# RetNet retention and an ELU feed-forward block: a new order for the first 35 microseconds of work

## The chip, the cores and the metric

The kernel runs on one core of one Trainium2 chip. The metric is the device time of one execution in microseconds, taken over several runs, with the median as its summary. The trace is of one profiled execution. The engines appear in it as PE (TensorE, matrix products; PEld is its weight load), DVE (VectorE), ACT (ScalarE), POOL (GpSimd) and SP (the sync queue, which issues all the transfers here).

## What is computed

A recurrent retention over 4 batches, 8 heads, 768 positions and head size 64 is followed by a feed-forward block with an ELU on 3072 tokens (model width 512, hidden width 2048). All data are float32, and the two weight matrices come in as float64.

```python
for t in range(S):
    state = gamma * state + k[:, :, t] (outer) v[:, :, t]
    y[:, :, t] = scale * q[:, :, t] @ state
x = y.transpose(0, 2, 1, 3).reshape(B * S, H * D)
h = x @ w_in
g = np.where(h > 0.0, h, np.exp(np.minimum(h, 0.0)) - 1.0)
return g @ w_out
```

## The kernel before

The tokens go in six blocks of 512. A block has four chunks of 128 positions. For two chunks at a time (a pair `pp`), retention runs in four steps: `scores` makes k-q products (L265) and DVE masks them in place (L270); `states` makes k-v products (L287) and sums them into running states, the first by an ACT copy (L296), the others by DVE additions (L298); `outputs` multiplies masked scores with v (L311), then states with q (L335, in two halves between which DVE reads one column of each bank into a tile `seen`, L323), and DVE multiplies the result with a decay table `etab` into `xb` (L342). `scale_v` multiplies v by decay factors: chunks 1 and 3 in eight small ACT instructions (L236), chunks 0 and 2 in one DVE instruction (L239), later ones on GpSimd.

The feed-forward weights come as 16 pieces of 1 MB in float64 bits. `load_piece` (L118) brings a piece into one of three staging buffers. `prepare` gives it to ACT (two instructions, L139 and L141, for each part), `decode` to DVE (four instructions for each part, L160 to L163), and the decode of a piece also issues the load of the piece three further on. `prepare(parts)` cuts a piece into that many parts by columns; `decode` is a generator that stops behind each part. Pieces 0 to 7 are the halves `w_a[n]`, `w_b[n]` of the first weight matrix for n = 0 to 3, pieces 8 to 15 belong to the second one.

Block 0 is computed with plain products, since the later blocks use a seven-product scheme that needs combined weights. `plain_first` makes 16 tiles of 128 hidden units by 512 tokens: for each n two tiles of `w_a[n]` and two of `w_b[n]`. Four of them are done in two halves of 256 tokens (L385), the first halves as soon as pair 0 has left `xb`, the second halves behind pair 1. They take four accumulation banks, a, a, b and d. The other twelve take all 512 tokens at once (L396). Each float32 product appears as two PE instructions. `elu` runs on ACT (L373, L374) and closes on DVE (L376). In the loop over these tiles a further piece is decoded behind every second one. `plain_second` then makes the output product for block 0 with one piece of the second matrix in each of eight rounds f (L410); DVE makes four sums of the piece in each round (L415), and the next decode follows. Within these rounds the retention of block 1 is placed too.

There is no scheduler: the order in which the code emits instructions is the order on each engine. The opening is written out by hand at L711 to L742. All loads stand in one queue on SP. It first issues piece 0, chunks 0 and 1, piece 1, chunks 2 and 3, and piece 2 (L173 to L179); `load` sends a chunk's transposed q and k (`qk`), then its plain k and v (`kvn`), 0.5 MB each. Before the tile loop starts, pieces 0, 1 and 2 have been decoded, in two, one and two parts.

Of the kernel before, what the change touches and what calls it, by code (L numbers as in the profile page):

```python
# [10 lines left out]
U32 = mybir.dt.uint32  # L11
# [5 lines left out]
def kernel(  # L17
# [30 lines left out]
    nc = tc.nc  # L48
    PSUM = bass.MemoryType.PSUM
    P = nc.NUM_PARTITIONS  # L50
# [8 lines left out]
    NCHUNK = NTOK // C  # L59
# [32 lines left out]
    chunks = [divmod(m, NCH) for m in range(NCHUNK)]  # L92
    raw = {}

    def load(m):

        if m >= NCHUNK:
            return
        qk = ldpool.tile([P, 2, HP, C], FP32, name="qk", tag="qk")
        nc.sync.dma_start(qk.rearrange("p a h c -> p (a h c)"), qkv[m, :, 0:1024])  # L100
        kv = ldpool.tile([C, 2, H, D], FP32, name="kvn", tag="kvn")
        nc.sync.dma_start(kv.rearrange("p a h c -> p (a h c)"), qkv[m, :, 1024:2048])
        raw[m] = (qk, kv)

# [3 lines left out]
    NPIECE = 2 * NQ + NF  # L110
    staged, prepared, decoded = [], [], []

    def load_piece():
        n = len(staged)
        if n < NPIECE:

            t = stage.tile([P, 1024, 2], U32, name="wraw", tag="stage")
            nc.sync.dma_start(t.rearrange("p c w -> p (c w)"), w_bits[n].bitcast(U32))  # L118
            staged.append(t)


# [2 lines left out]
    def prepare(parts=1):  # L124

        n = len(prepared)
        if n >= NPIECE:
            return
        t = staged[n]
        if n < 2 * NQ:  # L130
            dst = (w_a, w_b)[n % 2][n // 2].rearrange("p a b c d -> p (a b c d)")
        else:

            dst = w_s[n % NQ].rearrange("p a b c d -> p (a b c d)")[:, 0:1024]
        todo = []
        for part in range(parts):
            c = slice(part * 1024 // parts, (part + 1) * 1024 // parts)
            lo, hi, flat = t[:, c, 0], t[:, c, 1], dst.bitcast(U32)[:, c]
            nc.scalar.activation(flat, lo, AF.Copy, scale=2.0**-29)  # L139

            nc.scalar.activation(lo.bitcast(FP32), hi.bitcast(FP32), AF.Abs)  # L141
            todo.append((lo, hi, flat))
        prepared.append((dst, todo))
# [5 lines left out]
    def decode():  # L149

        n = len(decoded)
        if n >= NPIECE:
            return
        dst, todo = prepared[n]
        decoded.append(dst.rearrange("p (a b) -> p a b", a=2))
        vec = nc.vector
        for c, hi, flat in todo:
            cf = c.bitcast(FP32)

            vec.tensor_scalar(cf, cf, 122879.9921875, 2.0**-15, ALU.min, ALU.max)  # L160
            vec.tensor_scalar(c, c, 3, 0x3FFFFFF8, ALU.logical_shift_left, ALU.bitwise_and)
            vec.scalar_tensor_tensor(c, hi, 0xC0000000, c, ALU.bitwise_and, ALU.bitwise_or)
            vec.tensor_tensor(out=flat, in0=c, in1=flat, op=ALU.add)  # L163
            yield
        load_piece()
        if n >= 2 * NQ:
            nc.sync.dma_start(quarters(n - 2 * NQ)[:, 0:8], dst.rearrange("p (s c) -> p s c", c=P))

    def decode_all():
        for _ in decode():  # L170
            pass

    load_piece()  # L173
    load(0)
    load(1)
    load_piece()
    load(2)
    load(3)
    load_piece()  # L179


# [13 lines left out]
    etab = const.tile([P, 2, 2, S], FP32, name="etab")  # L195
# [33 lines left out]
    def scale_v(m):  # L229
        if m >= NCHUNK:  # L230
            return
        i = chunks[m][1]
        qk, kv = raw[m]
        if m in (1, 3):
            for h in range(H):
                nc.scalar.activation(kv[:, 1, h, :], kv[:, 1, h, :], AF.Copy, scale=vf[:, i, h : h + 1])  # L236
            return
        eng = nc.vector if m < CPB else nc.gpsimd
        eng.tensor_tensor(  # L239
            out=kv[:, 1], in0=kv[:, 1], in1=vf[:, i].unsqueeze(2).to_broadcast([C, H, D]), op=ALU.mult  # L240
        )
# [11 lines left out]
    def fresh(tb, n):  # L253

        return (tb * 2 * CPB + n) % (S // D) == 0

    def scores(tb, pp):

        two = [raw[tb * CPB + 2 * pp + x][0] for x in range(2)]
        sc = [ps_r.tile([P, 2, HP, D], FP32, name="sc", tag="r") for _ in range(2)]  # L260
        for x, qk in enumerate(two):
            for p in range(HP):
                for sub in range(2):
                    for a in range(2):
                        nc.tensor.matmul(  # L265
                            sc[a][rows(sub), x, p, :], lhsT=qk[rows(a), 1, p, rows(sub)],
                            rhs=qk[rows(a), 0, p, rows(sub)], start=True, stop=True, skip_group_check=True,
                        )
        for a in range(2):
            nc.vector.tensor_tensor(  # L270
                out=two[a][:, 1].rearrange("p h c -> p (h c)").rearrange("p (n t) -> p n t", t=D),
                in0=sc[a].rearrange("p x h t -> p (x h) t"),
                in1=cmask.unsqueeze(1).to_broadcast([P, 2 * HP, D]), op=ALU.mult,
            )

    def states(tb, pp):

        kvs = [ps_r.tile([P, 2, HP, D], FP32, name="kv", tag="r") for _ in range(2)]
        order = [(x, sub) for x in range(2) for sub in range(2)]
        last = lambda x, sub: fresh(tb, 4 * pp + 2 * x + sub + 1)  # L280
        for x in range(2):
            kv = raw[tb * CPB + 2 * pp + x][1]
            for p in range(HP):
                for sub in range(2):
                    for a in range(2):
                        if not last(x, sub):
                            nc.tensor.matmul(  # L287
                                kvs[sub][rows(a), x, p, :], lhsT=kv[rows(sub), 0, 2 * p + a, :],
                                rhs=kv[rows(sub), 1, 2 * p + a, :], start=True, stop=True, skip_group_check=True,
                            )  # L290
        for x, sub in order:
            n = 4 * pp + 2 * x + sub
            if last(x, sub):
                continue
            if fresh(tb, n):
                nc.scalar.copy(state(tb, n + 1), kvs[sub][:, x])  # L296
            else:
                nc.vector.tensor_tensor(out=state(tb, n + 1), in0=kvs[sub][:, x], in1=state(tb, n), op=ALU.add)  # L298
# [67 lines left out]
    def flush():  # L366
        while later:
            later.pop(0)()
# [9 lines left out]
    def plain_first():  # L378

        tiles = [(n, w, row, fi) for n in range(NQ) for w, row in ((w_a, 0), (w_b, 1)) for fi in range(2)]  # L380
        banks = [bank(x) for x in "aabd"]
        for t in range(2):
            for (n, w, row, fi), hp in zip(tiles, banks):
                for j in range(4):
                    nc.tensor.matmul(  # L385
                        hp[:, t, :], lhsT=w[n][:, fi, j // 2, j % 2, :], rhs=xb[:, j, half[t]],
                        start=(j == 0), stop=(j == 3), skip_group_check=True,
                    )
                if t == 1:
                    elu(g_plain[row * NF + 2 * n + fi], hp.rearrange("p a b -> p (a b)"))  # L390
                if t == 1 or fi == 1:
                    yield
        for n, w, row, fi in tiles[4:]:
            hp = ps_r.tile([P, TB], FP32, name="hp", tag="r")
            for j in range(4):
                nc.tensor.matmul(  # L396
                    hp, lhsT=w[n][:, fi, j // 2, j % 2, :], rhs=xb[:, j, :], start=(j == 0), stop=(j == 3)
                )
            elu(g_plain[row * NF + 2 * n + fi], hp)
            yield  # L400
        flush()

    def plain_second():

# [37 lines left out]
    def bank(x):  # L442
        return ps_f.tile([P, 2, TH], FP32, name="p" + x, tag=x, bufs=2 if x == "a" else 1)
# [264 lines left out]
            pass  # L708


    prepare(2)  # L711
    piece = decode()
    next(piece)
    scale_v(0)
    scale_v(1)
    scores(0, 0)
    next(piece)
    next(piece, None)
    states(0, 0)
    prepare()  # L720
    y = outputs(0, 0)
    next(y)
    next(y)
    next(y, None)
    scale_v(2)
    decode_all()
    scale_v(3)
    prepare(2)
    inner = plain_first()
    next(inner)  # L730
    scores(0, 1)
    states(0, 1)
    piece = decode()
    next(piece)
    next(inner)
    y = outputs(0, 1)
    next(y)
    next(y)
    next(y, None)
    next(piece)  # L740
    next(piece, None)
    prepare()  # L742
    for n, _ in enumerate(inner):
        if n % 2 == 1 and n < 15:
# [139 lines left out]
```

## Time and profile before

| what | us |
|---|---|
| median of 8 runs | 667.08 |
| lowest and highest of them | 664.66, 668.96 |
| profiled execution, whole | 667.51 |
| profiled execution, span of the trace | 665.5 |
| PE, DVE, ACT busy in the span | 640.9, 435.2, 228.3 |

A busy PE isn't PE at its peak, since the ends of matmuls are modelled. The mean granted clock of PE was 0.994 of full speed. At the start of the span the transfers dominate: the first chunk's scores begin at 7.43 us, the first tile's products at 20.03 us, and the twelve tiles with 512 tokens at 43.09 us.

### The profile page before, as it was taken

Reading aid. Unit: us, or ns where it says so; the run is one execution under the profiler, and the core shown is the slowest. Engines: PE = TensorE matmul, PEld = TensorE weight load, DVE = VectorE, ACT = ScalarE, POOL = GpSimd, SP = SyncE. Lnnn points to the kernel's source line nnn. Section 1 sums busy time; section 2 is a strip of 40 time slices with the busy share of each in tenths; the row PEclk is TensorE's granted clock in tenths of the full one; section 3 lists DMA queues with packets and bytes.
Section 4 is the critical chain, followed back from the end, with each engine's and each line's share of the span. In section 5 each row is a group of like instructions: output and inputs, shape, how many; then the busy total and the mean of one; then the engine's idle time right before and its main releaser. Section 6 shows DMA issues by size and latency. Waiting matters only on the chain.

```text
span 665.5 us, 14662 instructions
## 1 busy us (share of the span) xinstructions
PE 640.9 (96%) x6144; PEld 539.8 (81%) x6144; DVE 435.2 (65%) x769; ACT 228.3 (34%) x432; POOL 25.1 (4%) x28
## 2 busy tenths in 40 slices
PE   4889999999999999999999999999999999999997
PEld 4664444548888888889989888999889989888996
DVE  5688768656767744548856447867447858355874
ACT  7467642105441002543112454112455111445211
POOL 1000100000200000200000300000200000000000
PEclk9799999999999999999999999999999999999999
DMA  9538978449214757605767703777801768301693
GB/s 344 227 127 303 320 223 261 129 134 367 100 50 155 261 218 254 252 1 168 217 202 254 255 1 94 224 230 249 299 0 50 230 197 272 95 1 30 203 307 126
DMA packets 63825, 123.64 MB, mean 186 GB/s; under 512 B 5136, under 2 KB 22544, under 8 KB 61712
## 3 DMA queue, kind: packets, MB, share of 16 engines
q1 hardware_dynamic: 63760, 122.70, 55.9%
q8 instruction: 49, 0.80, 0.5%
q14 instruction: 16, 0.13, 0.0%
HBM read 100.66 MB, written 22.02 MB: 184 GB/s over the span
## 4 chain that ended last, share of the span: by engine, by line
PE 87%; DVE 8%; issue 2%; DMA 1%; ACT 0%; SPq 0%; DVEq 0%
PE pa L497 20%; PE pa L618 12%; PE pd L497 9%; PE pd L618 7%; PE hp L396 6%; PE pb L497 5%; PE pa L410 4%; PE pa L555 4%; DVE ts L607 3%; PE pb L618 2%; PE pd L555 2%; PE pd L410 2%; PE pb L410 2%; PE y L335 2%; PE sc L265 2%
## 5 line engine op out<-in xcount | busy, mean ns | idle before, releaser
L452 DVE TENSOR_TENSOR h<-pd,m 128x512 f32<-128x512 f32 x42 | 29.1, 692 | 86.0 <-ACT m L447 68.5
L447 ACT COPY m<-pa 128x512 f32<-128x512 f32 x63 | 36.3, 577 | 109.7 <-PE pa L497 73.7
L626 ACT COPY ms<-pa 128x128 f32<-128x128 f32 x84 | 22.3, 266 | 129.1 <-PE pa L618 124.6
L618 PE MATMUL pd<-ts,wq 128*128 128x128 f32 x448 | 60.3, 278 | 2.9 <-DVE res L630 2.9
L374 ACT ACTIVATE r<-r 128x512 f32<-128x512 f32 x96 | 60.5, 630 | 3.0
L618 PE MATMUL pa<-ts,wq 128*128 128x128 f32 x448 | 59.2, 275 | 0.0
L618 PEld LDWEIGHTS pd<-ts,wq 128*128 128x128 f32 x448 | 54.4, 192 | 4.6 <-DVE res L630 4.3
L373 ACT ACTIVATE r<-h 128x512 f32<-128x512 f32 x60 | 37.9, 631 | 57.2 <-DVE h L452 57.2
L618 PEld LDWEIGHTS pa<-ts,wq 128*128 128x128 f32 x448 | 54.8, 192 | 0.2
L618 PE MATMUL pa<-gC,wq 128*128 128x128 f32 x384 | 52.0, 278 | 0.4 <-ACT ms L626 0.4
L376 DVE SCALAR_TENSOR_TENSOR gC<-r,h 128x512 f32<-128x512 f32 x60 | 42.1, 702 | 10.8 <-ACT r L374 10.8
L618 PEld LDWEIGHTS pa<-gC,wq 128*128 128x128 f32 x384 | 47.2, 192 | 1.7 <-ACT ms L626 0.5
L239 POOL TENSOR_TENSOR kvn<-kvn,vf 128x512 f32<-128x512 f32 x20 | 23.1, 1153 | 457.4 <-DMA kvn<-in_qkv_dram 397.6
L497 PE MATMUL pa<-xb,w_s 128*128 128x256 f32 x160 | 37.8, 379 | 0.0
L497 PE MATMUL pa<-xb,w_a 128*128 128x256 f32 x160 | 37.8, 379 | 0.0
L497 PE MATMUL pa<-xt,w_s 128*128 128x256 f32 x160 | 37.8, 379 | 0.0
L497 PE MATMUL pa<-xt,w_b 128*128 128x256 f32 x160 | 37.8, 379 | 0.0
L497 PE MATMUL pd<-xt,w_b 128*128 128x256 f32 x160 | 37.8, 379 | 0.0
L497 PE MATMUL pb<-xb,w_a 128*128 128x256 f32 x160 | 37.8, 379 | 0.0
L497 PE MATMUL pd<-xt,w_s 128*128 128x256 f32 x160 | 37.8, 379 | 0.0
L630 DVE TENSOR_TENSOR res<-pd,ms 128x128 f32<-128x128 f32 x56 | 16.1, 287 | 31.3 <-PE pd L618 29.5
L497 PEld LDWEIGHTS pa<-xt,w_b 128*128 128x128 f32 x160 | 30.4, 190 | 4.1
(121 smaller groups left out, 1098.0 us busy)
## 6 DMA issues: line engine op xcount, KB each, us to landing
wq<-scratch_dram SPq DMA_DIRECT2D x196, 256.0 KB, 4.0
wraw<-in_w_dram SPq DMA_DIRECT2D x16, 1024.0 KB, 5.8
qk<-in_qkv_dram SPq DMA_DIRECT2D x24, 512.0 KB, 8.8
kvn<-in_qkv_dram SPq DMA_DIRECT2D x24, 512.0 KB, 9.4
scratch_dram<-so SPq DMA_DIRECT2D x22, 512.0 KB, 3.3
ws<-scratch_dram SPq DMA_DIRECT2D x7, 1024.0 KB, 7.8
scratch_dram<-w_s SPq DMA_DIRECT2D x8, 512.0 KB, 7.4
out_dram<-res SPq DMA_DIRECT2D x12, 256.0 KB, 3.7
```

The lines of the kernel that those rows point to most:

```text
L239: eng.tensor_tensor(out=kv[:, 1], in0=kv[:, 1], in1=vf[:, i].unsqueeze(2).to_broadcast([C, H, D]), op=ALU.mult)
L373: nc.scalar.activation(r, h, AF.Relu, scale=-1.0)
L374: nc.scalar.activation(r, r, AF.Exp, scale=-1.0)
L376: later.append(lambda: nc.vector.scalar_tensor_tensor(g, r, -1.0, h, ALU.add, ALU.max))
L396: nc.tensor.matmul(hp, lhsT=w[n][:, fi, j // 2, j % 2, :], rhs=xb[:, j, :], start=(j == 0), stop=(j == 3))
L410: nc.tensor.matmul(ops[d], lhsT=wo[:, row, d * P : (d + 1) * P], rhs=g_plain[row * NF + f], start=(f == 0 and row == 0), stop=(f == NF - 1 ...
L447: nc.scalar.copy(m, ps)
L452: nc.vector.tensor_tensor(out=h, in0=ps, in1=m, op=ALU.add)
L497: nc.tensor.matmul(ps[:, fi, :], lhsT=w[:, fi, j2, :], rhs=x[:, j2, :], start=(begin and fi == 0 and j2 == 0), stop=(j2 == 1), skip_group_ ...
L555: nc.tensor.matmul(ps[:, d, :], lhsT=ws[:, 2 * d + f // 4, f % 4, :], rhs=gq[INPUT2[j]][:, f, :], start=(begin and f == 0 and d == 0), sto ...
L618: nc.tensor.matmul(ps, lhsT=w[:, f, :], rhs=ts[j][k][:, f, :], start=(begin and f == 0), stop=(f == 3), skip_group_check=True,)
L626: nc.scalar.copy(m, ps)
```

## The change

The load of a chunk is split into its two transfers, so that the queue can send qk of two chunks before kv of either. The first issues become: qk0, qk1, kv0, kv1, piece 0 as two halves, piece 1, qk2, qk3, kv2, kv3, piece 2. v of chunk 0 is scaled on ACT and that of chunks 1, 2 and 3 on DVE. Pieces 0 and 1 are prepared and decoded in four parts each, and these parts are placed between the steps of retention; piece 2 is prepared in one part and is decoded inside the tile loop. Two tiles instead of four are done in halves of 256 tokens, in the two a banks, with a stop behind each half tile, and fourteen are done whole. A new function `busy` multiplies two ranges of columns of `etab` into bank b; nothing reads the result. It is called four times in the first pair of chunks.

```diff
+    def load_qk(m):
+        qk = ldpool.tile([P, 2, HP, C], FP32, name="qk", tag="qk")
+        nc.sync.dma_start(qk.rearrange("p a h c -> p (a h c)"), qkv[m, :, 0:1024])
+        raw[m] = [qk, None]
+    def load_kv(m):
+        kv = ldpool.tile([C, 2, H, D], FP32, name="kvn", tag="kvn")
+        nc.sync.dma_start(kv.rearrange("p a h c -> p (a h c)"), qkv[m, :, 1024:2048])
+        raw[m][1] = kv
...
-    def load_piece():
+    def load_piece(parts=1):
...
-            nc.sync.dma_start(t.rearrange("p c w -> p (c w)"), w_bits[n].bitcast(U32))
+            for part in range(parts):
+                c = slice(part * 2048 // parts, (part + 1) * 2048 // parts)
+                nc.sync.dma_start(t.rearrange("p c w -> p (c w)")[:, c], w_bits[n].bitcast(U32)[:, c])
...
+    load_qk(0)
+    load_qk(1)
+    load_kv(0)
+    load_kv(1)
+    load_piece(2)
     load_piece()
-    load(0)
-    load(1)
-    load_piece()
-    load(2)
-    load(3)
+    load_qk(2)
+    load_qk(3)
+    load_kv(2)
+    load_kv(3)
     load_piece()
...
-        if m in (1, 3):
+        if m == 0:
...
-        banks = [bank(x) for x in "aabd"]
+        banks = [bank("a") for _ in range(2)]
...
-                if t == 1 or fi == 1:
-                    yield
-        for n, w, row, fi in tiles[4:]:
+                yield
+        for n, w, row, fi in tiles[2:]:
...
+    def busy(columns):
+        ps = bank("b").rearrange("p a b -> p (a b)")
+        nc.tensor.matmul(ps[:, 0:columns], lhsT=etab[:, 0, 0, 0:P], rhs=etab[:, 0, 1, 0:columns], start=True, stop=True)
...
-    prepare(2)
+    scale_v(0)
+    scores(0, 0)
+    scale_v(1)
+    prepare(4)
     piece = decode()
     next(piece)
-    scale_v(0)
-    scale_v(1)
-    scores(0, 0)
+    states(0, 0)
+    y = outputs(0, 0)
+    next(y)
+    busy(512)
+    busy(256)
+    next(y)
+    next(piece)
+    busy(256)
+    next(y, None)
+    busy(256)
+    next(piece)
     next(piece)
     next(piece, None)
-    states(0, 0)
-    prepare()
-    y = outputs(0, 0)
-    next(y)
-    next(y)
-    next(y, None)
-    scale_v(2)
-    decode_all()
-    scale_v(3)
-    prepare(2)
+    prepare(4)
+    piece = decode()
     inner = plain_first()
     next(inner)
+    scale_v(2)
     scores(0, 1)
+    scale_v(3)
+    next(inner)
+    next(piece)
     states(0, 1)
-    piece = decode()
-    next(piece)
-    next(inner)
     y = outputs(0, 1)
     next(y)
     next(y)
     next(y, None)
-    next(piece)
-    next(piece, None)
+    for _ in piece:
+        pass
     prepare()
```

## The prediction

> **What bounds the kernel now.** I read the chain of waits first, because it says which engine sets the end. TensorE holds 87% of it.
>
> ```profile
> PE 87%; DVE 8%; issue 2%; DMA 1%; ACT 0%; SPq 0%; DVEq 0%
> ```
>
> So only time in which TensorE is idle or slow can be won. The busy times by stage show where that is (columns: stretch, its length, then busy us and instructions of PE, PEld, DVE, ACT, POOL; granted clock, DMA share, GB/s).
>
> ```profile
> 0.00:18.50 18.50, 7.99 (x240) 7.47 (x240) 9.76 (x38) 11.97 (x21) 2.00 (x8) 1.00 0.91 352
> 18.50:25.60 7.10, 5.69 (x20) 4.48 (x14) 5.65 (x7) 4.78 (x13) 0.00 (x0) 0.52 0.73 278
> 25.60:43.30 17.70, 15.96 (x309) 13.72 (x308) 12.52 (x23) 6.64 (x9) 0.00 (x0) 1.00 0.33 118
> 43.30:84.40 41.10, 41.10 (x97) 18.15 (x96) 32.82 (x39) 28.79 (x39) 4.44 (x4) 1.00 0.84 287
> 84.40:148.50 64.10, 64.10 (x609) 31.77 (x608) 46.04 (x80) 14.25 (x15) 0.14 (x1) 1.00 0.61 182
> ```
>
> From 43.30 to 148.50 TensorE has no gap. All that the change can win lies ahead of 43.3, and nothing after it may be lost. The same chain in order of time (start, length, what) shows the opening's links:
>
> ```profile
> 2.11 7.86 DMA qk<-in_qkv_dram
> ...
> 16.75 1.36 issue
> ...
> 20.03 6.39 PE pa L385 x16
> ...
> 34.74 1.30 DVE xb L342 x2
> ...
> 36.08 3.72 PE pa L385 x16
> ```
>
> The reader is to see that the opening waits for the second chunk's qk, that TensorE once had no instruction to run (1.36 us, no wait shown), and that the same 16 matmuls took 6.39 us at the halved clock and 3.72 at full clock: 2.67 us lost. The timeline gives the links between, and two pairs in the output product that matter later:
>
> ```profile
> 11.20 1.29 DVE L270 TENSOR_TENSOR qk<-sc,cmask 128x512 f32<-128x512 f32 x2 [1.12 <-PE sc L265]
> 13.90 0.37 ACT L296 COPY xt<-kv 128x256 f32<-128x256 f32 x1 [0.56 <-PE kv L287]
> 14.66 1.34 DVE L298 TENSOR_TENSOR xt<-kv,xt 128x256 f32<-128x256 f32 x3
> 18.68 1.29 DVE L342 TENSOR_TENSOR xb<-y,etab 128x512 f32<-128x512 f32 x2 [2.43 <-PE y L335]
> ...
> 90.57 1.23 DVE L163 CUSTOM_DVE_ANT_0 w_s<-wraw,w_s 128x2048 uint16<-128x2048 uint16 x1
> ...
> 136.76 0.42 DVE L415 TENSOR_TENSOR so<-w_s 128x256 f32<-128x256 f32 x1
> ...
> 141.65 1.88 PE L410 MATMUL pa<-gC,w_s 128*128 128x512 f32 x4
> ```
>
> [...] The trace agrees on the fall and on the rise 5.5 us after dense work began at 20.03. It shows 1.00 before the first transition, but 64 small matmuls take 1.90 us at 13.57 and 1.16 at 32.02, so I read the whole opening as half clock. [...] L160 takes 0.42 us at 512 columns and 0.69 at 1024, L162 0.69 and 1.23.
>
> **Loads.** Transfers land nearly in order of issue, so I read landings off position. The first 1 MB landed at 5.7, and the sync queue's waits put the next at 7.4, 8.7 (1, 1.5, 2 MB); chunk 1's qk and v waits end at 10.0 and 11.3. In the new order: qk0 4.4 (5.7 less one step of 1.3), qk1 5.7, kv0 7.4, kv1 8.7, the halves of piece 0 at 10.0 and 11.3, piece 1 about 14, chunks 2 and 3 by 20.3, piece 2 at 22.8. There is one issue more (0.47 us on SP, hidden behind full DMA engines). The waits show that the ninth issue waits for the first landing, and so on; the twelfth will wait for kv1 (8.7), harmless.
>
> **First chunk pair.** Scores end at 6.85 instead of 11.2. DVE masks them by 8.2 (1.29) and scales v1 when kv1 is there, to 9.4 (0.69). ACT scales v0 from 7.4 to 9.5 (2.02). States run to 10.5, products with v to 12.2. Then the new bound: prepare(4) stands ahead of the state copy on ACT. Its eight instructions at 256 columns are not in the trace; from 0.66 (512) and 1.16 (1024) they come to 0.40 each (at most 0.66, at least 0.29 by halving 1024 twice). 10.0 + 8 x 0.39 = 13.1, copy to 13.5 (before: 14.27). Three state sums on DVE: 14.9 (before 16.0). The first two unread products (512 and 256 columns) need 1.3 us at full clock, 2.6 at half (L385: 0.216 per 256-column instruction, two per product), so they end at 13.5 to 14.8, inside the wait for 14.9. Corrections, the "seen" copies (0.25), then one decode part on DVE, which now stands before L342: four instructions of about 0.29, 0.29, 0.42, 0.42 plus starts, 1.45. L342 ends at 18.3; at half clock the third unread product and the corrections are late and it is 18.95. Before: 20.0. The 1.36 us instruction gap I take as gone, since TensorE reaches its first instructions 3 us sooner [...]; if it stays, L342 is up to 1.3 later. Call the end of L342 X.
>
> **Second pair, from X.** DVE carries it: parts 3 and 4 (2.9), scale 2 (0.69), masks (1.3), scale 3 (0.65), first part of piece 1 (1.45), states (1.75), "seen" and corrections (1.0), L342 (1.3): X + 11.05. TensorE's two half tiles (1.73 each), scores and states fit between. The two ACT scales that become DVE ones add 0.69 each to this chain and free 2.02 of ACT each, which nobody waits for. Then two second halves (3.46) and two w_b[0] tiles at 512 columns (3.43 each): X + 21.4. Working whole instead of by halves is worth 0.03 a tile. The four tiles that before were done at 43.26 are done at 39.8 (X = 18.35): 3.5 us won. Without the clock, the first half tile costs 3.45 and holds the scores: about 41.6 to 42.3, 1.0 to 1.7 won.
>
> **Afterwards.** One decode fewer lies done ahead of the loop, so each piece is decoded two tiles ahead of use instead of four. Splitting adds 1.9 us of DVE for piece 1 and 1.3 for piece 0 (5.8 against 3.9 and 4.5), piece 2 saves 0.6. Piece 2 ends at X + 20.0 and its tile starts at X + 21.4: hidden by 1.4. Later ones have about 4 us. Piece 4 is loaded at 33.8 instead of 24.4; landing 5 us later it meets ACT at 41, 2 us spare. Nothing else stands behind these loads on SP until chunk 4. In the output product each f needs the piece decoded behind f - 1. At f = 1: the decode ended at 91.80 (90.57 + 1.23) where f = 1 started at 91.16; that decode was the next one, now it is the one needed: 0.66 lost. At f = 7: sums from 136.76 (1.46), decode 3.94: 142.16 against 141.65: 0.53 lost. The others have 2 to 4 us. Sum: 1.2 back.
>
> **Sum.** 3.5 - 1.2 = 2.3 us off 667.51, the profiled execution's time (span 665.5, 2.0 around it): 665.2. That execution lies 0.43 above the median of 667.08, inside the spread of 664.66 to 668.96, so I leave the forecast at 665.2.
>
> **Rivals.** (1) The unread products don't raise the clock in time: in the trace six microseconds of small matmuls did not. For it: they are 1.1 us of work at full clock, spread out. Against: at half clock they fill 2.6 us without a gap. 667.51 - 1.35 + 1.2 = 667.4. (2) Instruction supply stops TensorE again in the chain: X + 1.3, 666.5. (3) Slower: the shorter lead. If each decode ends s later against TensorE than worked out, f = 1 and f = 7 cost 1.2 + 2s and piece 2 costs s - 1.4. The win is gone at s = 1.1; at s = 2.0 it is 5.8 against 3.5: 669.8. For it: one L161 took 1.41 us instead of 0.70 at 63.08, beside a GpSimd multiply. Against: it was one in many.
>
> **Numbers.** A change below 0.3% (2.0 us) can't be told from none here. Chances: forecast 0.57, rival 1 0.20, rival 2 0.10, slower 0.13. The forecast's own range is 663.3 to 667; its middle lies at the 0.3% line (665.08), so a little over two thirds of it, leaning to unseen gains, counts as faster: 0.40. Same: 0.17 of it, with rivals 1 and 2, and a little of the last: 0.48. Slower: 0.12. The range 663.3 to 668 takes in rivals 1 and 2 and leaves out most of the last.
>
> **What would show it.** Right: first sc matmuls near 4.4, L296 near 13.1 behind prepare, L342's end near 18.4, L385 at 0.216 us an instruction from its first, a wait of 0.5 to 0.7 at L410 on L163 twice. Wrong: granted clock 0.50 after X; L265 waiting past 6; more than two waits of TensorE between 43 and 145; a wait of L396 on a decode.

## The result, and the profile after

| | median us | lowest to highest | runs |
|---|---|---|---|
| before | 666.62 | 663.54 to 668.96 | 32 |
| after | 670.80 | 668.56 to 672.09 | 11 |

The changed kernel takes 1.0063 of the time before (95% interval 1.0048 to 1.0079): about 4.2 us more, where 2 us less had been forecast. The profiled execution after took 668.48 us (span 666.0), the shortest of its twelve. A second profile of each kernel was taken with the experiments, and both are used below. The line numbers of the changed kernel differ: L265 is L278 there, L287 is L300, L296 and L298 are L309 and L311, L311 is L324, L335 (the products of states with q, called corrections) is L348, L342 is L355, L385 is L398, L396 is L408, L410 is L427, and L163 is L172. The unread products are L418.

The shares of the chain of waits, after:

```profile
PE 85%; DVE 11%; issue 2%; DMA 1%; ACT 1%; SPq 0%; DVEq 0%; ACTq 0%
```

VectorE has 11% of it instead of 8%. The busy times by the same stretches, after (columns as in the prediction):

```profile
0.00:18.50 18.50, 11.53 (x248) 8.92 (x248) 9.56 (x41) 13.43 (x31) 2.00 (x8) 1.00 0.90 344
18.50:25.60 7.10, 7.07 (x212) 5.96 (x212) 6.77 (x17) 2.36 (x2) 0.00 (x0) 1.00 0.79 290
25.60:43.30 17.70, 14.79 (x98) 9.20 (x95) 14.36 (x29) 6.24 (x9) 0.00 (x0) 0.90 0.27 96
...
84.40:148.50 64.10, 62.97 (x606) 30.94 (x605) 49.62 (x84) 15.64 (x16) 0.00 (x0) 1.00 0.66 194
```

The reader is to see that the second stretch got its full clock (1.00 instead of 0.52), that the third lost it (0.90 instead of 1.00), and that the last one has gaps in TensorE now (62.97 of 64.10, before 64.10). The chain in order of time (start, length, what) shows the third stretch:

```profile
26.89 1.03 issue
...
29.38 1.30 DVE xb L355 x2
...
30.73 5.28 PE pa L398 x16
```

TensorE stood still for 1.03 us in which the profile shows nothing that it waited for ("issue"; called an instruction gap from here on), waited for `xb`, and then took 5.28 us for 16 matmuls that took 3.72 at full clock in the profile of before. Its waits over the whole span (us in total, times, longest) hold two of another kind:

```profile
PE pa L427 <- DVE w_s L172: 1.1, 2, 0.6
PE y L348 <- issue: 1.0, 1, 1.0
```

### The profile page after: what moved, and what is told of

Same layout as the page of the kernel before. It is cut to its first block, busy times and chain, and to the rows that moved or that the text cites. A ratio compares the mean times of both kernels' runs of the same rounds, so it can differ in the third digit from the quotient of the medians.

```text
span 666.0 us, 14672 instructions
## 1 busy us (share of the span) xinstructions
PE 644.9 (97%) x6136; PEld 538.0 (81%) x6136; DVE 437.4 (66%) x786; ACT 227.6 (34%) x432; POOL 23.6 (4%) x28
## 4 chain that ended last, share of the span: by engine, by line
PE 85%; DVE 11%; issue 2%; DMA 1%; ACT 1%; SPq 0%; DVEq 0%; ACTq 0%
PE pa L514 20%; PE pa L635 12%; PE pd L514 9%; PE hp L408 7%; PE pd L635 7%; PE pb L514 5%; PE pa L572 4%; PE pa L427 3%; DVE ts L624 3%; PE pb L635 2%; PE pd L572 2%; PE kv L300 2%; PE y L348 2%; PE y L324 2%; PE sc L278 2%
## 5 line engine op out<-in xcount | busy, mean ns | idle before, releaser
L252 POOL TENSOR_TENSOR kvn<-kvn,vf 128x512 f32<-128x512 f32 x20 | 21.6, 1080 | 461.3 <-DMA kvn<-in_qkv_dram 457.6
L514 PE MATMUL pa<-xb,w_s 128*128 128x256 f32 x160 | 37.8, 379 | 0.0
L514 PE MATMUL pa<-xb,w_a 128*128 128x256 f32 x160 | 37.8, 379 | 0.0
L514 PE MATMUL pa<-xt,w_s 128*128 128x256 f32 x160 | 37.8, 379 | 0.0
L514 PE MATMUL pb<-xb,w_a 128*128 128x256 f32 x160 | 37.8, 379 | 0.0
L514 PE MATMUL pd<-xt,w_s 128*128 128x256 f32 x160 | 37.8, 379 | 0.0
L514 PE MATMUL pa<-xt,w_b 128*128 128x256 f32 x160 | 37.8, 379 | 0.0
L514 PE MATMUL pd<-xt,w_b 128*128 128x256 f32 x160 | 37.8, 379 | 0.0
L514 PEld LDWEIGHTS pa<-xt,w_b 128*128 128x128 f32 x160 | 30.4, 190 | 4.1
```

What stands on the lines that cost most here:

```text
L252: eng.tensor_tensor(out=kv[:, 1], in0=kv[:, 1], in1=vf[:, i].unsqueeze(2).to_broadcast([C, H, D]), op=ALU.mult)
L514: nc.tensor.matmul(ps[:, fi, :], lhsT=w[:, fi, j2, :], rhs=x[:, j2, :], start=(begin and fi == 0 and j2 == 0), stop=(j2 == 1), skip_group_ ...
```

## The experiments

Two theories stood at the start. The first: the time is lost to the clock of TensorE and to its instruction gaps in the opening. The rival: it is lost to the shorter lead of the decodes, that is, to pieces that are decoded one step later before their use than they were. Each run was timed beside the kernel before on the same chip, and the ratio is given with its 95% interval. Where "main loop" is said, the first matmul of the seven-product scheme (L497, after: L514) is meant.

**The changed kernel again.** No edit.

> The changed kernel again, for a second profile. The profile at hand is one of its two fastest executions (668.5 us at a mean clock of 0.997; the others 669.8 to 672.1 at 0.993 to 0.995). Clock theory: an execution at 0.994 has a further 3 to 4 us at half clock ahead of 45 us, in the first pair of chunks too, and so starts its whole tiles 2 us later than the first profile did (35.8). Rival, instruction supply: the clock is as in the first profile and the 2 us are gaps in which TensorE has no instruction.

Measured: 669.33 us against 665.54, ratio 1.0048 (1.0030 to 1.0067). The chain of this second profile, in order of time:

```profile
26.65 1.23 issue
...
30.69 6.36 PE pa L398 x16
37.05 23.17 PE hp L408 x54
```

The first tile was at full clock again, so the half clock expected in the first pair isn't there. The whole tiles start 1.0 us later than in the first profile (37.05, 36.01), not 2, and nearly all of that is the clock in the second pair: 6.36 us instead of 5.28. Busy time and granted clock of TensorE for single microseconds of this profile show how it came (stretch, length, busy us and instructions, clock, DMA share, GB/s):

```profile
26.00:27.00 1.00, 0.53 (x5) 1.00 0.00 0
27.00:28.00 1.00, 0.12 (x6) 1.00 0.00 0
28.00:29.00 1.00, 0.74 (x38) 1.00 0.07 16
29.00:30.00 1.00, 0.28 (x20) 0.62 0.00 0
30.00:31.00 1.00, 0.31 (x1) 0.50 0.00 0
...
36.00:37.00 1.00, 1.00 (x6) 0.97 1.06 147
```

After some 3.2 us in which TensorE was busy for about half the time, in pieces, the clock falls to 0.50 (a mean of 0.62 in that microsecond puts the fall at 29.2). It comes back 5.4 us after dense work began at 30.7; in the first profile after it took 3.2. The fall comes at 29.2 here and near 30.5 in the first profile, with the same program; what sets the moment isn't shown. Up to the fall TensorE never stood still for longer than 1.23 us here (the instruction gap) and 1.18 there (29.32 to 30.50, waiting for `xb`), counted from 26.

**Without the unread products.**

```diff
-    busy(512)
-    busy(256)
...
-    busy(256)
...
-    busy(256)
```

> The changed kernel without its four unread products. If they keep the clock up: the first half tile takes 3.5 us instead of 1.7, and the time rises by 1 to 2.5 us. If they are worth nothing [...]: within 0.7 us. If they hold the corrections up (the first profile shows TensorE going straight from them to the corrections): up to 1 us faster.

Measured: 668.50 us, ratio 1.0044 (1.0029 to 1.0059). The chain:

```profile
18.69 3.78 PE pa L398 x8
...
32.47 3.72 PE pa L398 x16
```

The expectation named three ways, and the second is nearest, in a form that it didn't foresee. The first half tile does take 3.78 us instead of 1.7. But TensorE came back to full clock from 24 us on and kept it through the second pair, where the 16 matmuls took 3.72 us. The unread products moved the half clock from the first tile to a later one, and the times are not told apart.

**One more decode in the tile loop.**

```diff
-        if n % 2 == 1 and n < 15:
+        if n % 2 == 1:
```

> The changed kernel with one more decode in the tile loop, behind its last tile, so that each round of the output product finds its piece decoded a round ahead, as before. Shorter lead theory: both waits of TensorE on L172 go (0.63 and 0.50 us, with restarts 1.55 us between the first and last of these rounds) and the time falls by 1.2 to 1.6 us. Rival: the waits move to another round or to the tile in front, and the time stays within 0.4 us.

Measured: 667.83 us, ratio 1.0034 (1.0019 to 1.0049), a median 1.5 us lower than that of the changed kernel on the same chip. The intervals overlap, so the traces decide: from the first L427 to the main loop it is 65.8 us in the first profile after (83.9 to 149.7) and in the second, and 64.2 here (85.4 to 149.5), with no wait of L427 on L172 left. Before it was 64.2 (84.3 to 148.5). The shorter lead costs 1.6 us.

**The kernel before with the unread products alone.**

```diff
     y = outputs(0, 0)
     next(y)
+    busy(512)
+    busy(256)
     next(y)
+    busy(256)
     next(y, None)
+    busy(256)
```

> The kernel before with the four unread products alone, at the same places in the first pair. If they raise the clock in time: the first 16 matmuls of L385 take 3.7 us instead of 6.4 and the time falls by 1 to 2.7 us. If they stand in the way (at half clock they take 2.6 us where the state sums are ready 0.7 us behind L311): 0.5 to 2 us slower. If neither: within 0.5 us.

Measured: 665.65 us, ratio 0.9995 (0.9982 to 1.0009). TensorE's part of the timeline of this run (start, length, line, what, count, and in brackets the idle time before it with its releaser):

```profile
15.54 2.23 PE L406 MATMUL pb<-etab 128*128 128x512 f32 x4
17.70 0.68 PE L335 MATMUL y<-qk,xt 64*64 64x64 f32 x24
...
21.05 3.72 PE L385 MATMUL pa<-xb,w_a 128*128 128x256 f32 x16 [0.80 <-DVE xb L342]
```

Both halves of the expectation came true and cancelled. The tile is at full clock, 3.72 us, and it starts at 21.05 instead of 20.03 or 19.22 (the two profiles without the products), since they stood in front of the corrections, whose inputs were ready.

**The kernel before again.** No edit.

> The kernel before, unchanged, for a second profile and for the granted clock of each of its executions. If the profile of before was an unlucky one: most executions have a mean clock above 0.996 and end near 665, and the 2.7 us of the slow first tile are paid by a minority, so that there was less to win than the profile showed. If it was typical: most are at 0.994.

Measured: 665.45 us, ratio 0.9998 (0.9980 to 1.0015). The chain of this second profile of before:

```profile
16.88 0.42 issue
...
19.22 3.72 PE pa L385 x16
...
33.57 3.72 PE pa L385 x16
...
40.74 19.31 PE hp L396 x45
```

No tile was at half clock and the instruction gap at the same place was 0.42 instead of 1.36 us. The whole tiles start at 40.74 instead of 43.26. Of 14 executions eight had a mean clock of 0.996 or more. That is between the two outcomes expected: the profile that the forecast rested on, at 0.994, was of an execution worse than most, and this one (663.77 us at a mean clock of 1.000) is near the fastest. The 2.5 us between them are not there to be won in every execution.

**Unread products in the second pair.**

```diff
     y = outputs(0, 1)
     next(y)
+    busy(512)
     next(y)
     next(y, None)
+    busy(512)
+    busy(256)
```

> The changed kernel with three more unread products in the second pair of chunks: 512 columns behind its products with v, 512 and 256 behind its last corrections, where TensorE stands idle between 26.6 and 30.7 us. If the fall of the clock in this stretch is what the change loses: the 16 matmuls of L398 behind it take 3.7 us instead of 5.3 to 6.8 in all three profiles so far, and the time falls by 1.5 to 2.8 us. If the cause is the emptier second pair itself or the shorter lead: within 0.7 us.

Measured: 667.92 us, ratio 1.0036 (1.0019 to 1.0053); 13 of 22 executions had a mean clock of 0.999 or 1.000, which none of the 25 executions of the changed kernel had. The median lies 1.4 us below that of the changed kernel, measured earlier on another chip, just short of the range expected, and the intervals overlap. The chain of this run's profile:

```profile
29.57 1.96 PE pb L418 x2
...
32.80 3.62 PE pa L398 x16
```

The 16 matmuls take 3.62 us. But this is one of the slower executions (670.18 us), and its clock fell all the same, from 29.6 to 33.0: it was the unread products that ran in it (1.96 us for two instructions, where the next run has 1.88 for four). From the first tile to the first L427 it took 65.8 us, no less than the 65.4 of the first profile after. So what the products do is seen in the clock of most executions and in the next run, not in this trace.

**Both repairs.** The one more decode and the products in the second pair, both edits as above.

> The changed kernel with both repairs: one more decode in the tile loop, and the three unread products in the second pair. If the shorter lead and the fall of the clock are two separate losses, they add up: 2.5 to 3.2 us below the changed kernel, 666 to 667, and what is left against the kernel before (about 1 us) is TensorE's idle time in the second pair. If they overlap: 667.5 or more.

Measured: 665.73 us against 665.84, ratio 1.0002 (0.9985 to 1.0020). This interval and that of the changed kernel (1.0048 to 1.0079) lie apart. TensorE's timeline:

```profile
19.45 1.99 PE L398 MATMUL pa<-xb,w_a 128*128 128x256 f32 x8 [1.05 <-DVE xb L355]
...
30.23 1.88 PE L418 MATMUL pb<-etab 128*128 128x512 f32 x4
31.95 3.62 PE L398 MATMUL pa<-xb,w_a 128*128 128x256 f32 x16
```

The waits on L172 are gone and the clock stays. The ratio is 1.0063 and 1.0048 with no repair, 1.0034 or 1.0036 with one and 1.0002 with both, so the two losses are separate and add up, as far as the intervals tell. The median lies a little below the range, and the 1 us that had been expected to remain isn't seen in it. It is there all the same. This profile and the second one of before (first tile at 19.22, shown above) both have full clock from the first tile to the main loop. Their output products, of this run and then of before (the two times are the first and the last start):

```profile
L427 PE MATMUL pa<-gC,w_s x64: 592/592/697, 83.5 to 145.5; 128*128 128x512 f32 x64
...
L410 PE MATMUL pa<-gC,w_s x64: 592/592/697, 81.8 to 143.8; 128*128 128x512 f32 x64
```

From the first tile to the first of them it is 64.0 us here and 62.6 in before. The median hides this, because the repaired kernel has the better clock: 16 of its 22 executions have a mean of 0.999 or 1.000, with 665.4 us in the mean, against 3 of 43 of before beside them, with 664.2. So the repairs don't undo the whole loss; in part the unread products pay for it with a clock that before seldom has.

**Tiles and second pair as before.** Loads and first pair as changed; from there the four tiles by halves and the decodes of before.

```diff
...
-        banks = [bank("a") for _ in range(2)]
+        banks = [bank(x) for x in "aabd"]
...
-    prepare(4)
-    piece = decode()
+    prepare()
+    scale_v(2)
+    decode_all()
+    scale_v(3)
+    prepare(2)
     inner = plain_first()
     next(inner)
-    scale_v(2)
     scores(0, 1)
-    scale_v(3)
-    next(inner)
-    next(piece)
     states(0, 1)
+    piece = decode()
+    next(piece)
+    next(inner)
...
```

> Loads and first pair as changed, with the unread products; from the second pair on as before: piece 1 decoded whole, piece 2 in two parts ahead of the tile loop, four tiles by half the tokens, chunk 3's v scaled on ACT. If the second pair and the lead are where the change loses: the first pair's 1.5 us are kept, L427's waits go, and the time is 664 to 665.5, 4 to 5 us below the changed kernel and at or below the kernel before. If the loads or the first pair lose it: 667.5 or more.

Measured: 666.01 us against 665.34, ratio 1.0016 (0.9999 to 1.0032), above the range expected. The change's loss is gone, its win isn't there. 11 of 22 executions had a mean clock of 0.999 or 1.000, so with the half tiles put back the clock stays up about as often as with the three unread products (13 of 22). TensorE waits for the decode of piece 1, which stands behind the four parts of piece 0 on VectorE:

```profile
PE pb L398 <- DVE w_b L172: 1.4, 1, 1.4
```

**The same without the unread products.** The edit is that of the run without them.

> The same without the unread products. [...] the unread products are worth the slow first tile alone: 1 to 2.7 us slower than with them. If they only moved the time at half clock elsewhere: within 0.7 us.

Measured: 665.49 us, ratio 1.0006 (0.9988 to 1.0024). Here the first tile took 6.58 us, as at half clock (6.39 in the first profile of before), and the time is no higher. For the third time the unread products took what they gave.

**States ahead of the preparation of piece 0**, on the version just shown.

```diff
-    prepare(4)
-    piece = decode()
-    next(piece)
     states(0, 0)
+    prepare(4)
+    piece = decode()
+    next(piece)
```

> As the run with tiles as before and without unread products, and the states of the first pair emitted ahead of prepare(4), so that ACT's state copy no longer stands behind eight instructions for piece 0. If that copy is what holds the first pair: L309 starts near 11.2 instead of 13.9, the state sums end near 12.6, xb is ready 1 to 2 us sooner (18.7 before) and the time falls by 1 to 1.8 us, to about 664, below the kernel before. If the decode of piece 0 takes its place as what the first tile waits for: within 0.5 us.

Measured: 666.38 us against 665.84, ratio 1.0016 (1.0001 to 1.0031). ACT's and then TensorE's part of the timeline:

```profile
11.39 0.37 ACT L309 COPY xt<-kv 128x256 f32<-128x256 f32 x1 [1.41 <-PE kv L300]
...
17.69 6.00 PE L398 MATMUL pa<-xb,w_a 128*128 128x256 f32 x16 [1.51 <-ACT wraw L150]
```

The copy is 2.4 us sooner than in the version just shown (13.78), so it had stood behind the preparation. The first tile starts 1.0 us sooner, and takes 6.00 us. The time didn't fall. VectorE's decode parts now stand between the corrections, TensorE waits 1.6 us there, and 1.5 more ahead of the first tile. The profile puts that wait down to an ACT instruction for piece 1 that ended at 17.59, but the tile doesn't read its output; the `xb` that it does read was ready at 17.55, 1.1 us sooner than in the version just shown (18.66). The clock was 0.50 from 15.5 to 22.4 us.

**The same with unread products put into its gaps, and the changed kernel with everything together.** Added to the last: `busy(512)` behind the scores, `busy(512)` behind the first corrections, `busy(512)` and `busy(256)` behind the last ones.

> The run with states ahead of prepare(4) and tiles as before, with unread products put back, but only where its profile shows TensorE idle: 512 columns behind the scores, 512 behind the first corrections, 512 and 256 behind the last ones. If the half clock took back what the earlier xb won there (its first tile took 6.0 us): that tile takes 3.7 to 4.5 us and the median falls by 1 to 2 us, to 664.5 to 665.4, below the kernel before on the same chip. If unread products always take as much as they give: within 0.5 us of it.

> The changed kernel with both repairs (one more decode in the tile loop, unread products in the second pair), states ahead of prepare(4), and the first pair's unread products at the places of the other run. If the state copy behind prepare(4) holds the changed kernel's first pair: xb is ready 1 to 1.5 us sooner and the time falls by as much against the run with both repairs, to 0.2% below the kernel before. If not: no difference from before, as that run.

Measured: 666.58 us, ratio 1.0019 (1.0002 to 1.0036), and 666.20 us, ratio 1.0009 (0.9990 to 1.0028), both against 665.61. In both the hoped-for win is missing, and the other outcome named came true: 0.2 us from the run with states ahead, and no difference from before. TensorE's timeline in the first of them:

```profile
16.72 2.35 PE L419 MATMUL pb<-etab 128*128 128x512 f32 x4
18.87 4.88 PE L398 MATMUL pa<-xb,w_a 128*128 128x256 f32 x16
```

The last unread products took 2.35 us, against 1.88 for the same four in the run with both repairs, and lasted longer than the wait for `xb` (L355 ends at 18.15); the tile starts 1.2 us later than without them and takes 4.88 us, still more than 3.72. No version tried beats the kernel before.

## Why the prediction was wrong

**The step that failed** is the second pair: "X + 11.05" and, behind it, "X + 21.4 ... done at 39.8 ... 3.5 us won". The sum asked for the clock at the first tile and took it as kept from there on. The same sum left TensorE idle through part of the second pair, since one half tile stood ahead of the scores instead of two, and none ahead of the products with v instead of two. Behind these gaps the clock was down: 5.28 and 6.36 us for the 16 matmuls instead of 3.72; with the gaps filled, 13 and 16 of 22 executions had a mean clock of 0.999 or 1.000, against none of 25. The instruction gap that was "taken as gone" came back in that pair, 1.03 and 1.23 us, so that it lasted 12.2 and 12.4 us instead of 11.05. From X to the first L427 it took 65.4 and 66.7 us (18.5 to 83.9, 18.3 to 85.0); the prediction's own terms give 21.4 + 41.2 = 62.6. The slower matmuls (1.6 and 2.6) and the longer pair (1.2 and 1.3) make up the difference.

**A wrong reading** stood behind it. The prediction read "the whole opening as half clock" and had the unread products raise it; that they would was the author's estimate, since no run had had them yet. In the first profile of before, the trace's record of the clock begins with a rise at 15.22, falls at 18.63 and rises again at 25.46, and the matmuls agree: 24 of L335 take 0.73 us, near the 0.68 of full clock.

```profile
15.31 0.73 PE L335 MATMUL y<-qk,xt 64*64 64x64 f32 x24
```

So the clock had risen with nothing but small matmuls on TensorE up to then, against what rival 1 says, and it fell behind the instruction gap of 1.36 us; in the second profile, where that gap was 0.42 us, it rose at 14.1 and didn't fall. The loss that then struck the second pair, a fall behind gaps, stood in the profile that was being costed. What the products in the first pair are seen to do is keep the clock. In all seven profiles that have them at these places it doesn't fall ahead of the first tile, which in six of them takes 1.99 us for 8 matmuls, or 3.72 and 4.04 for 16; in four of the five without them it takes 3.78 for 8 or 6.00 to 6.58 for 16, and in the fifth 3.72.

**Against the kernel before** the clock is not what differs. The mean over 25 executions of the changed kernel is 0.9951, over 196 of before 0.9955. The half clock was moved from the first tile to the second pair; this is why the win counted for it did not come, and no reason to be slower than before. What is lost is the lead, 1.6 us, and 1.4 us of the second pair at full clock (64.0 less 62.6, with the three unread products in it, which weren't taken out at full clock). X gives back 0.8. A further part lies outside the traced span: whole time less span is 2.5 us in the mean of both sets of the changed kernel and 2.1 in those of before, and 2.1 again with both repairs; why is open. That makes some 2.6 of the 3.8 us between the medians timed together, as an estimate, and the rest isn't found.

**The baseline** was mis-sized too. "3.5 us won" was counted from 43.26, where the first profile of before began its whole tiles. The second profile has 62.6 us from its first tile to the first L410 (19.2 to 81.8), just what the changed kernel would have needed at its best. That the profiled time lay only 0.43 above the median of the first eight hid it: executions of before at its clock of 0.994 take 666.5 us in the mean, while 139 of the 196 lie at 0.995 or above, at 666.0 or less. The second profile, at 663.77, errs to the other side. Of the win only X remained, and X is 0.7 to 0.9 us sooner than in that profile, not 1.65.

**Right:** the state copy behind `prepare(4)` at 13.1 (13.60), and its cause, shown by the run with the states ahead; X at 18.35 (18.47); a tile at full clock from the first matmul; the places of the two lost waits, f = 1 and f = 7. Their size was 1.2 us in the sum and is 1.6 in the traces: 0.63 and 0.50 of waiting, and the rest within the busy time around the restarts.

**Rival 3**, slower through the shorter lead, has its sign and its mechanism, but not the size that it needed: s was about 0, each later decode had room, and no tile of the loop waited for one. **Rival 1** named the clock and put it at the wrong pair. **Rival 2**, instruction supply, is a part of it as far as the gaps go (1.03 and 1.23 us); that supply is what they come from isn't shown.

The account of the second profiles, after less before, span 666.3 less 661.8 = 4.5 us: first tile 0.9 sooner (18.3, 19.2); from there to the first L427 4.1 more (66.7, 62.6); the rounds of the output product 1.6 more (65.8, 64.2); from the main loop to the end 0.3 less (515.6, 515.9). Of the 4.1, 2.6 are half clock that this execution of before happened not to have.

Not settled: why the versions with tiles as before keep nothing of an earlier X. Their profiles show a stretch at half clock or a late decode in each case, and no run separates them. What decides the length of the instruction gaps (0.4 to 2.0 us, in each profile) wasn't tried; the last section says where they end.

## What to carry to other kernels

Before a stall in one profile is counted as something to win, a second profile of the same kernel should show it; half clock in an opening can be there in one execution and not in the next (6.39 and 3.72 us for the same 16 matmuls of before). Work that looks like mere order, such as half tiles between two dependent steps, can go with a clock that stays full (11 of 22 executions with them put back, none of 25 without), so a change that takes it away has to be costed with the clock in every gap that it leaves, not only in the first. And a decode that was done a round ahead is a buffer, worth 1.6 us here: where it is spent in the opening, look for the round far behind it that will find its input late. Last, when a repair brings the median back, the clock of the executions and a pair of profiles at equal clock tell whether it undid the loss or paid for it with something else.

## What was not expected of the hardware

The granted clock of one and the same program varied widely. Over 196 executions of the kernel before, timed beside the experiments, the mean clock ran from 0.988 to 1.000: 17 at 0.992 took 668.2 us in the mean, 113 at 0.995 to 0.997 took 665.4, and 22 at 0.999 or 1.000 took 663.7. That is a spread of 4.5 us that goes with the clock, as much as the change did. (The record of the clock begins with its first rise, at 9.5 to 24.6 us in the profiles; the mean counts what lies ahead of that as full.)

The half clock came in stretches of two lengths. Leaving out the one at the very end of each, the 14 profiles hold 12 stretches of it behind the first rise, six of 3.41 us (30.5 to 33.9 in the first profile after) and six of 6.83 (18.6 to 25.5 in the first of before). In the 3.4 us ahead of each, as long as a short one, TensorE was busy for 33 to 61%, and no pause was longer than 2.0 us. That alone doesn't decide: in the second profile of before 3.4 us from 29.9 on were busy for 37%, and no fall followed. Two of the 12 came in the middle of the work, at 337.8 us (the run without the unread products) and 534.8 (unread products in the second pair), behind instruction gaps of 1.71 and 1.97 us.

The instruction gaps have a mark in common. The 14 profiles hold 45 of them of 0.3 us or more, and each ends 1.2 to 1.6 us behind the end of a 16 KB transfer on the queue that the profile calls instruction (1.47 for the gap of 1.36 in the first profile of before, 1.25 for that of 1.03 in the first after).

Unread products aren't free even inside a wait. In the first of the last two runs one of 512 columns took 2.07 us at 7.6 us and 1.13 at 13.2, and behind the first of them the k-v products began at 9.61 instead of the 8.36 of the run without it: a filler sized by its shorter time held up the work behind it.
